# The product of q with k^T v by two 64-row halves of TensorE in two PSUM banks

## The chip, the cores and the metric

The kernel runs on one core of a Trainium2 chip. Its engines run side by side: TensorE (PE in the profile, its weight loads PEld), VectorE (DVE), ScalarE (ACT), GpSimd (POOL) and SyncE (SP), which issues most DMAs. The metric is the device time of one execution in microseconds (us); lower is better. The time before is the median of three runs.

## The reference

Three layers follow one another on 2304 tokens (batch of 4, 8 heads, 576 positions, 64 values a head). The first is a linear attention with an RMS norm, the second and third are MoE layers of plain matrix products.

```python
kv = np.einsum('bhsd,bhse->bhde', k, v)
out = np.einsum('bhsd,bhde->bhse', q, kv)
rms = np.sqrt(np.mean(out * out, axis=-1, keepdims=True) + 1e-06)
x = out / rms * g_norm                                  # to (2304, 512)
h = np.maximum(np.maximum(x @ w1, x @ w2), x @ w3)      # d_ff = 768
x = h @ w_out
for e in range(4):                                      # experts, 1024 wide
    out += p[:, e:e+1] * (np.maximum(x @ ew1[e], 0) @ ew2[e])
```

## The kernel before

Everything is float32. The change lies in the first stage, the attention, which takes some 85 us; the two MoE stages take the rest and are matrix products on TensorE almost without a break.

The 2304 tokens form ten groups. Eight are full (0, 1, 3, 4, 5, 6, 8, 9): 256 positions of one batch, two for each partition. Groups 2 and 7 are pair groups: the last 64 positions of two batches, 128 tokens. For each batch, `att_kv` (steps K, line 282) accumulates k^T v of each head, 64x64, in PSUM bank 7; copies bring it to SBUF as `kvb`. `att_T` (steps T, line 308) transposes q into `qT`: with two positions to a partition, a tile of 128 partitions holds one head's 64 values of the first position and the 64 values of the second one below them. `att_O` (steps O) multiplies `qT` with `kvb`. In a full group it is one matmul a head (line 332): all 128 rows against a 128x128 block of `kvb` that holds the head's k^T v twice on its diagonal, zeros elsewhere, so that both positions come out side by side. The blocks' zeros are set once by a memset of `kvb` on GpSimd. Heads 0 to 3 go to one PSUM bank and heads 4 to 7 to a second one. A pair group needs one bank (line 324).

On the product follow: squares by ACT from each bank (line 345), sums of them on VectorE (line 346), the root on ACT (`att_N`, line 354), its reciprocal and refinement on VectorE (lines 355 to 358), and the scale, by VectorE, of each bank with the reciprocal (line 365). The product stays in its banks until then. `att_X` (line 374) transposes the scaled tokens, and the result goes with the factor of g_norm to `yT` (lines 378 and 380); `split_x` (line 388) divides it into a high and a low part for the MoE products (`col_mm`, line 260). In between, VectorE converts the MoE weights (lines 232 to 236).

Two things set the order of the work. One is a string of steps, written by hand: each engine runs its instructions in the order in which the steps issue them (a letter and its numbers: O4 is the product of group 4, A000 the first MoE product). The other is the PSUM banks: banks 0 to 3 are handed out in turn to products (`bank("acc")`), banks 4 to 6 in turn to transposes and the first MoE products. In the profile and in the orders below, `bank0_66` to `bank7_73` are the banks 0 to 7.

```python
turn[kind] += 1
return banks[(turn[kind] - 1) % 4 if kind == "acc" else 4 + (turn[kind] - 1) % 3]
```

The products come in the order O1, O0, O3, O2, O4, O6, O5, O8, O7, O9 and take the banks 0 and 1, 2 and 3, 0 and 1, 2, 3 and 0, 1 and 2, 3 and 0, 1 and 2, 3, 0 and 1.

Of the kernel before, what the change touches and what calls it, by code (L numbers as in the profile page):

```python
# [21 lines left out]
def tile_attn_moe_moe2(  # L22
# [23 lines left out]
    nc = tc.nc  # L46
# [139 lines left out]
    place = list(range(N1))  # L186
    place[12], place[22] = 22, 12
# [40 lines left out]
    def conv1(pool, key):  # L228
        cpos[2] += 1
        words = stage.pop(key).bitcast(I32).rearrange("p (n t) -> p n t", t=2)  # L230
        ti = conv[key].bitcast(I32)
        nc.vector.tensor_scalar(out=ti, in0=ti, scalar1=3, scalar2=None, op0=ALU.logical_shift_left)
        nc.vector.scalar_tensor_tensor(
            out=ti, in0=words[:, :, 0], scalar=29, in1=ti, op0=ALU.logical_shift_right, op1=ALU.bitwise_or
        )
        nc.vector.scalar_tensor_tensor(
            out=ti, in0=words[:, :, 1], scalar=-(2**31), in1=ti, op0=ALU.bitwise_and, op1=ALU.bitwise_or
        )


    cpos = [0, 0, 0]

    def conv2(key, eng="ap"):
        w, t = new_w(key), conv.pop(key)
        split_h(w, t, eng[0])
        split_l(nc.gpsimd if eng[1] == "p" else nc.vector, w, t, key)
        if key[0] == "a":
            nc.sync.dma_start(out=w_d[key], in_=t)

    def load_w_to(pool, n):  # L250
        while cpos[0] < min(n, N1):
            load_w(pool, worder[cpos[0]])
            cpos[0] += 1
# [18 lines left out]
    def att_kv(kvb, b, c, eng=""):  # L272
# [22 lines left out]
    def att_T(pool, gi, eng="aa"):  # L295

# [4 lines left out]
        if pair:  # L301
            qr = pool.tile([P, 2, H, D], F32, tag="qr", name="qr", bufs=1)
            nc.gpsimd.tensor_copy(out=qr, in_=qs.rearrange("p h r d -> p r h d"))
        for i in range(2):
# [4 lines left out]
            copy(eng[i], t[:, :, :, i] if pair else t[:, i], ps)  # L309
        qT[gi] = t  # L310

    def att_O(pool, kvb, gi):
        b, s0, _ = groups[gi]
        qt = qT[TAIL] if s0 is None else qT.pop(gi)
        ps = [bank("acc") for i in range(1 if s0 is None else 2)]
        xt = pool.tile([P, 2, H, D], F32, tag="xt", name=f"xt{gi}", bufs=3)
        if s0 is None:
            nbank = 1
            for c in range(NPAIR):
                for bb in range(2):  # L320
                    rows = slice(bb * HALF, (bb + 1) * HALF)
                    toks = slice((b + bb) * P // B, (b + bb + 1) * P // B)
                    pair = kvb[(b + bb) % 2][:, 2 * c * P : 2 * c * P + 384]
                    nc.tensor.matmul(
                        ps[0][rows, c * P : (c + 1) * P], qt[:, c, toks, :],
                        pair.rearrange("p (h n) -> p h n", h=2)[:, :, 0:D], start=True, stop=True,
                    )
            dst = [xt[:, 0]]
        else:
            nbank = 2  # L330
            for h in range(H):
                nc.tensor.matmul(
                    ps[h // 4][:, h % 4 * P : (h % 4 + 1) * P], qt[:, h // 4, h % 4, :],
                    kvb[b % 2][:, h * P : (h + 1) * P], start=True, stop=True,
                )
# [939 lines left out]
```

## Time and profile before

| | |
|---|---|
| median of 3 runs | 1098.17 us (1097.75 to 1099.57) |
| profiled execution, its own time | 1097.36 us |
| span of its trace | 1095.6 us |
| mean granted clock of TensorE | 0.994 |
| busy: PE, PEld, DVE, ACT, POOL | 98%, 96%, 70%, 54%, 20% of the span |

The rows of the trace name an engine, a line of the kernel, the operation with its output and input, and the time in us. A wait stands in brackets behind a row, with what ended it. Matmuls overlap, so the length of a row of several is its stretch from the first to the last end. A float32 matmul appears as two passes, each with its weight load. A shape such as `128*64 128x64` gives the rows and columns of the tile of TensorE, and then the output or the operand.

### The profile page before, as it was taken

How to read it: one execution, taken by the hardware profiler on the slowest of the kernel's cores; microseconds unless marked ns; L12 is line 12 of the kernel's file. 1: busy time of each engine (PE TensorE's matmuls, PEld its weight loads, DVE VectorE, ACT ScalarE, POOL GpSimd, SP SyncE). 2: the span in 40 equal slices, each digit the busy share in tenths (PEclk: the TensorE clock that was granted, in tenths of full speed). 3: DMA queues.
4: the chain of work that ended last, by engine and by line, in shares of the span. 5: the costliest groups of instructions: out<-in, count | busy, mean ns of one | idle time of the engine just before them, and what ended most of it. 6: DMA issues, size and time to landing. Idle time of an engine off the chain costs nothing.

```text
span 1095.6 us, 19209 instructions
## 1 busy us (share of the span) xinstructions
PE 1069.1 (98%) x7318; PEld 1051.1 (96%) x7318; DVE 765.7 (70%) x1424; ACT 593.8 (54%) x1257; POOL 221.9 (20%) x269
## 2 busy tenths in 40 slices
PE   7889999999999889999999999999999999999998
PEld 7789999999999789999999999999999999999997
DVE  3889985667656878776766666667677576666556
ACT  3554234435343767665665666666566566556652
POOL 1334422330101101112111211212212220221121
PEclk8999999999999999999999999999999999999999
DMA  9955545431511977288579579659849956956875
GB/s 258 302 157 186 152 177 207 141 116 35 196 58 49 343 262 285 91 316 251 87 242 268 104 193 281 163 117 289 230 77 296 266 88 225 276 113 166 234 223 116
DMA packets 109820, 209.17 MB, mean 191 GB/s; under 512 B 13856, under 2 KB 67104, under 8 KB 109728
## 3 DMA queue, kind: packets, MB, share of 16 engines
q1 hardware_dynamic: 89248, 169.34, 46.3%
q0 software_dynamic: 19472, 37.76, 19.4%
q8 instruction: 57, 0.93, 0.3%
q10 hardware_dynamic: 1008, 0.85, 0.3%
q14 instruction: 35, 0.29, 0.1%
HBM read 137.93 MB, written 69.99 MB: 190 GB/s over the span
## 4 chain that ended last, share of the span: by engine, by line
PE 63%; DVE 0%; issue 0%; DVEq 0%
PE bank L877 32%; PE bank L616 31%; DVE wr L578 0%; DVE xr L499 0%; DVE fa L860 0%; DVE hr L652 0%; DVE hr L650 0%; DVEq L1270 0%
## 5 line engine op out<-in xcount | busy, mean ns | idle before, releaser
L877 PE MATMUL bank<-wr 128*128 128x256 f32 x1701 | 263.5, 283 | 0.4 <-DVE wr L578 0.4
L877 PEld LDWEIGHTS bank<-wr 128*128 128x128 f32 x1701 | 239.8, 190 | 0.6 <-DVE wr L578 0.6
L616 PE MATMUL bank<-rb,wl 128*128 128x384 f32 x1032 | 211.7, 341 | 4.4 <-DVE rb L499 2.5
L670 ACT ACTIVATE fa<-bank 128x384 f32<-128x384 f32 x192 | 94.7, 493 | 171.4 <-PE bank L616 169.5
L616 PEld LDWEIGHTS bank<-rb,wl 128*128 128x128 f32 x1032 | 176.1, 189 | 7.7 <-DVE rb L499 3.7
L616 PE MATMUL bank<-xr,wl 128*128 128x384 f32 x864 | 175.9, 338 | 1.7 <-DVE xr L499 1.1
L616 PEld LDWEIGHTS bank<-xr,wl 128*128 128x128 f32 x864 | 144.9, 188 | 3.7 <-DVE xr L499 2.5
L652 DVE TENSOR_TENSOR wr<-fa,wr 128x384 fp32r<-128x384 f32 x131 | 72.5, 553 | 50.8 <-ACT wr L645 50.6
L877 PE MATMUL bank<-wr,hr 128*128 128x256 f32 x558 | 91.1, 281 | 0.0
L835 POOL DMA_DIRECT2D out_dram<-w2s x48 | 48.1, 1027 | 190.4 <-DVE ob L860 143.4
L835 POOL DMA_DIRECT2D out_dram<-ob x48 | 47.7, 1033 | 170.8 <-DVE w2s L860 89.8
L877 PEld LDWEIGHTS bank<-wr,hr 128*128 128x128 f32 x558 | 80.6, 189 | 0.0
L645 ACT ACTIVATE wr<-fa 128x384 fp32r<-128x384 f32 x152 | 78.2, 529 | 2.0 <-DVE fa L660 0.5
L877 PE MATMUL bank<-wr,xr 128*128 128x256 f32 x405 | 67.9, 281 | 0.0
L759 DVE TENSOR_TENSOR fa<-bank,fa 128x384 f32<-128x384 f32 x54 | 30.0, 555 | 51.3 <-ACT fa L756 36.0
L693 DVE TENSOR_TENSOR fa<-bank,fa 128x384 f32<-128x384 f32 x48 | 26.8, 558 | 49.0 <-PE bank L616 49.0
L682 DVE TENSOR_TENSOR fa<-bank,fa 128x384 f32<-128x384 f32 x48 | 26.8, 558 | 48.0 <-ACT fa L670 47.1
L858 ACT ACTIVATE ob<-bank,p_all 128x256 f32<-128x256 f32 x102 | 48.4, 474 | 21.7 <-PE bank L877 20.0
L858 ACT ACTIVATE w2s<-bank,p_all 128x256 f32<-128x256 f32 x104 | 49.3, 475 | 18.6 <-PE bank L877 18.6
L616 PE MATMUL bank<-op,wl 128*128 128x384 f32 x288 | 58.7, 339 | 0.6 <-ACT fa L670 0.6
L835 POOL DMA_DIRECT2D out_dram<-fa x37 | 34.2, 1054 | 123.3 <-DVE fa L860 69.5
L877 PEld LDWEIGHTS bank<-wr,xr 128*128 128x128 f32 x405 | 59.0, 188 | 0.0
(206 smaller groups left out, 2020.6 us busy)
## 6 DMA issues: line engine op xcount, KB each, us to landing
rb<-op_d SPq DMA_DIRECT2D x42, 768.0 KB, 4.7
xr<-op_d SPq DMA_DIRECT2D x42, 768.0 KB, 6.6
out_dram<-w2s POOLq DMA_DIRECT2D x47, 256.0 KB, 5.8
out_dram<-ob POOLq DMA_DIRECT2D x46, 256.0 KB, 5.4
op<-op_d SPq DMA_DIRECT2D x14, 768.0 KB, 7.8
stage_a<-in_moe_w_dram SPq DMA_DIRECT2D x18, 512.0 KB, 4.0
w1s<-in_moe_w_dram SPq DMA_DIRECT2D x30, 256.0 KB, 3.6
out_dram<-fa POOLq DMA_DIRECT2D x30, 256.0 KB, 6.0
```

Source lines behind the costliest of these rows:

```text
L616: nc.tensor.matmul(out, w[wi][:, c * P : (c + 1) * P], y[yi][:, c, :], start=(i == 0 and k in begin), stop=(i == 5), skip_group_check=k no ...
L645: nc.scalar.activation(out=ops[key][0], in_=src, func=AF.Relu if relu else AF.Copy)
L652: nc.vector.tensor_tensor(out=lo, in0=src, in1=f32(hi), op=ALU.subtract)
L670: nc.scalar.activation(out=out, in_=in_, func=func)
L682: nc.vector.tensor_tensor(out=t22, in0=x, in1=t22, op=ALU.add)
L693: nc.vector.tensor_tensor(out=t12, in0=x, in1=t12, op=ALU.add)
L759: nc.vector.tensor_tensor(out=mx[done] if i == 0 else t, in0=x, in1=t, op=ALU.add)
L835: nc.gpsimd.dma_start(out=rows, in_=src, accum_op=ALU.add)
L858: nc.scalar.activation(out=o, in_=piece(ps, i), func=AF.Copy, scale=pe)
L877: nc.tensor.matmul(piece(ps, i), h[hi][:, i * P : (i + 1) * P], w[wi], start=fresh, stop=last, skip_group_check=True,)
```

## The change

In a full group each head's product is now two matmuls, each on 64 rows of TensorE: the first position of all tokens on rows 0 to 63 into the first bank, the second on rows 64 to 127 into the second bank, one after the other in turn. `kvb` no longer has blocks with zeros: it holds each k^T v in both halves of the partitions, 128x512, by as many copies as before, and the two memsets are gone. A pair group uses two banks as well: even heads go to the first, odd heads to the second, by tiles of 64 rows and 64 columns; its square, sum and scale become two each, of 128x256. The result of the scale is written in the order of the tokens, contiguous. `bank("acc")` is called twice by each pair group, so the turn of the banks shifts: O1, O0, O3, O2, O4, O6, O5, O8, O7, O9 take the banks 0 and 1, 2 and 3 alternately.

The string of steps is written out in smaller steps (the square by O, the sum o, the root N, the refinement m n r, the scale M, and so on, loads included). The instructions keep the order that they had on each engine, the loads of SP too, but for what follows from the counts above; the load of g_norm now stands ahead of the first loads of v on ACT's queue. Three buffers of MoE weights move to a tile `wx` of their own, and the swap of two buffers (`place`) is gone.

```diff
-    place = list(range(N1))
-    place[12], place[22] = 22, 12
...
-        if c == NPAIR - 1:
-            dst = kvb[b % 2][:, 0 : H * P].rearrange("p (c h n) -> p c h n", h=2, n=P)
-            for h in range(2):
-                src = ps[h * D : (h + 1) * D, 0 : NPAIR * D].rearrange("p (c e) -> p c e", e=D)
-                e = eng[2 * h :] or "aa"
-                copy(e[0], dst[0:D, :, h, 0:D], src)
-                copy(e[1], dst[D:P, :, h, D:P], src)
+    def att_J(kvb, b, eng="aaaa"):
+        dst = kvb[b % 2].rearrange("p (c h e) -> p c h e", h=2, e=D)
+        for h in range(2):
+            src = kv_ps[b][h * D : (h + 1) * D, 0 : NPAIR * D].rearrange("p (c e) -> p c e", e=D)
+            for i in range(2):
+                copy(eng[2 * h + i], dst[i * D : (i + 1) * D, :, h, :], src)
 
...
     def att_O(pool, kvb, gi):
         b, s0, _ = groups[gi]
-        qt = qT[TAIL] if s0 is None else qT.pop(gi)
-        ps = [bank("acc") for i in range(1 if s0 is None else 2)]
+        pair = s0 is None
+        qt = qT[TAIL] if pair else qT.pop(gi)
+        ps = [bank("acc") for i in range(2)]
         xt = pool.tile([P, 2, H, D], F32, tag="xt", name=f"xt{gi}", bufs=3)
-        if s0 is None:
-            nbank = 1
+        half = [slice(i * D, (i + 1) * D) for i in range(2)]
+        if pair:
             for c in range(NPAIR):
-                for bb in range(2):
-                    rows = slice(bb * HALF, (bb + 1) * HALF)
-                    toks = slice((b + bb) * P // B, (b + bb + 1) * P // B)
-                    pair = kvb[(b + bb) % 2][:, 2 * c * P : 2 * c * P + 384]
+                for i in range(2):
+                    for bb in range(2):
+                        toks = slice((b + bb) * P // B, (b + bb + 1) * P // B)
+                        nc.tensor.matmul(
+                            ps[i][half[bb], c * D : (c + 1) * D], qt[half[i], c, toks, :],
+                            kvb[(b + bb) % 2][half[i], (2 * c + i) * D : (2 * c + i + 1) * D], start=True, stop=True,
+                        )
+        else:
+            for h in range(H):
+                for i in range(2):
                     nc.tensor.matmul(
-                        ps[0][rows, c * P : (c + 1) * P], qt[:, c, toks, :],
-                        pair.rearrange("p (h n) -> p h n", h=2)[:, :, 0:D], start=True, stop=True,
+                        ps[i][:, h * D : (h + 1) * D], qt[half[i], h // 4, h % 4, :],
+                        kvb[b % 2][half[i], h * D : (h + 1) * D], start=True, stop=True,
                     )
-            dst = [xt[:, 0]]
-        else:
-            nbank = 2
-            for h in range(H):
-                nc.tensor.matmul(
-                    ps[h // 4][:, h % 4 * P : (h % 4 + 1) * P], qt[:, h // 4, h % 4, :],
-                    kvb[b % 2][:, h * P : (h + 1) * P], start=True, stop=True,
-                )
-            dst = [xt[:, :, 4 * i : 4 * i + 4, :].rearrange("p r h d -> p h r d") for i in range(2)]
-        o = [ps[i].rearrange("p (n d) -> p n d", d=D) for i in range(nbank)]
-
-        def small(nm):
-            return smp.tile([P, nbank, 8], F32, tag=nm, name=f"{nm}{gi}")
-
-        ss = small("ss")
-        for i in range(nbank):
-            sq = xt[:, i]
-            nc.scalar.activation(out=sq, in_=o[i], func=AF.Square)
-            nc.vector.reduce_sum(out=ss[:, i, :], in_=sq, axis=AX.X)
-        xtok[gi] = (xt, ss, o, dst, small)
-
-    def att_N(gi):
-        xt, ss, o, dst, small = xtok[gi]
-        nbank = len(o)
-        s0, rr = small("s0"), small("rr")
-
+        n = 4 if pair else 8
+        dst = [xt[:, 0].rearrange("p (c h) d -> p h c d", h=2)[:, i] if pair else xt[:, i] for i in range(2)]
+        o = [ps[i][:, : n * D].rearrange("p (h d) -> p h d", d=D) for i in range(2)]
+        for i in range(2):
+            nc.scalar.activation(out=dst[i], in_=o[i], func=AF.Square)
+
+        xtok[gi] = [xt, o, dst] + [smp.tile([P, 2, n], F32, tag=nm, name=f"{nm}{gi}") for nm in ("ss", "s0", "rr")]
+
+    def att_sum(gi):
+        dst, ss = xtok[gi][2:4]
+        for i in range(2):
+            nc.vector.reduce_sum(out=ss[:, i, :], in_=dst[i], axis=AX.X)
+
+    def att_root(gi):
+        ss, s0, rr = xtok[gi][3:]
         nc.scalar.activation(out=s0, in_=ss, func=AF.Sqrt, scale=1.0 / D, bias=eps)
         nc.vector.reciprocal(out=rr, in_=s0)
-        nc.vector.scalar_tensor_tensor(out=rr, in0=ss, scalar=EPS * D, in1=rr, op0=ALU.add, op1=ALU.mult)
-        nc.vector.scalar_tensor_tensor(out=rr, in0=rr, scalar=1.0 / D, in1=s0, op0=ALU.mult, op1=ALU.add)
-        nc.vector.reciprocal(out=rr, in_=rr)
-        for i in range(nbank):
-            by = rr[:, i, :].unsqueeze(2).to_broadcast([P, 8, D])
-            src = o[i]
-            if nbank == 2:
-                by = by.rearrange("p (h r) d -> p h r d", r=2)
-                src = src.rearrange("p (h r) d -> p h r d", r=2)
-            nc.vector.tensor_tensor(out=dst[i], in0=src, in1=by, op=ALU.mult)
...
-        kvb = [att.tile([P, H * P + P], F32, name=f"kvb{i}", bufs=1) for i in range(2)]
-        for t in kvb:
-            nc.gpsimd.memset(t, 0.0)
...
+        kvb = [att.tile([P, H * D], F32, name=f"kvb{i}", bufs=1) for i in range(2)]
...
-            "K00 K01 c0 d0 K02 K03 T1.va O1 T0.vv N1 K10 K11 O0 X1 N0 T2 T3.va K12 K13.vvaa X0.va O3 S0.pv "
-            "N3 O2 K20 T4 O4 s0.pp N2 T5 N4 K21 c1 T6.av K22 c2 K23 X2 X3 d1 d2 O6 O5 s1.pp K30 s2.pp N6 N5 "
+            "K13 J1.vvaa Lk30 X0 x0.va O3 o3 S0.p z0.v N3 m3 n3 r3 M3 O2 o2 K20 T4 t4 O4 o4 s0.p l0.p N2 m2 n2 "
+            "r2 M2 T5 t5 N4 m4 n4 r4 M4 K21 Lk31 Lq8 Lw3 Lq9 c1 T6 t6.av K22 c2 K23 J2 X2 x2 X3 x3 d1 e1 g1 Lw4 "
...
```

The first place is TensorE's order at the product of group 4 (its q in `qT4`), behind a k^T v product and two transposes of q. Before:

```order
L282 MATMUL bank7_73<-v2_0_276,k2_0_273 64x64 x10
L308 MATMUL bank4_70<-ident_74,q4_239 128x128 x4
L308 MATMUL bank5_71<-ident_74,q4_239 128x128 x4
L332 MATMUL bank3_69<-kvb1_174,qT4_500 128x128 x4
L332 MATMUL bank0_66<-kvb1_174,qT4_500 128x128 x4
L308 MATMUL bank6_72<-ident_74,q5_241 128x128 x4
```

And after the change:

```order
L322 MATMUL bank3_69<-kvb1_178,qT2_407 64x64
L280 MATMUL bank7_73<-v2_0_278,k2_0_275 64x64 x10
L305 MATMUL bank4_70<-ident_74,q4_241 128x128 x4
L305 MATMUL bank5_71<-ident_74,q4_241 128x128 x4
L329 MATMUL bank0_66<-kvb1_178,qT4_538 128x64
L329 MATMUL bank1_67<-kvb1_178,qT4_538 128x64
```

Before, O4 filled bank 3 first and then bank 0; now its matmuls write the banks 0 and 1 in turn.

The second place is TensorE's order at the product of group 9, between MoE products of the first weights (`xr`, `wl`). Before:

```order
L260 MATMUL bank4_70<-xr_81,wl_83 128x384 x12
L260 MATMUL bank5_71<-xr_81,wl_83 128x384 x12
L332 MATMUL bank0_66<-kvb1_174,qT9_785 128x128 x4
L332 MATMUL bank1_67<-kvb1_174,qT9_785 128x128 x4
L260 MATMUL bank6_72<-xr_81,wl_83 128x384 x12
L374 MATMUL bank4_70<-ident_74,xt7_853 128x128 x4
```

And after the change:

```order
L322 MATMUL bank1_67<-kvb0_177,qT2_407 64x64
L322 MATMUL bank1_67<-kvb1_178,qT2_407 64x64
L258 MATMUL bank4_70<-xr_81,wl_83 128x384 x12
L258 MATMUL bank5_71<-xr_81,wl_83 128x384 x12
L329 MATMUL bank2_68<-kvb1_178,qT9_846 128x64
L329 MATMUL bank3_69<-kvb1_178,qT9_846 128x64
```

O9 went to banks 0 and 1, and now goes to banks 2 and 3, in turn.

The third place is VectorE's order at the scales of group 3 (`xt3`), with the sums of groups 2 and 4 behind them. Before:

```order
L357 SCALAR_TENSOR_TENSOR rr3_470<-rr3_470,s03_469 128x16
L358 RECIPROCAL rr3_470<-rr3_470 128x16
L365 TENSOR_TENSOR xt3_453<-bank0_66,rr3_470 128x4x2x64
L365 TENSOR_TENSOR xt3_453<-bank1_67,rr3_470 128x4x2x64
L346 TENSOR_REDUCE ss2_487<-xt2_478 128x8
L346 TENSOR_REDUCE ss4_520<-xt4_511 128x8 x2
```

And after the change:

```order
L356 SCALAR_TENSOR_TENSOR rr3_492<-rr3_492,s03_491 128x16
L358 RECIPROCAL rr3_492<-rr3_492 128x16
L364 TENSOR_TENSOR xt3_471<-bank0_66,rr3_492 128x512
L364 TENSOR_TENSOR xt3_471<-bank1_67,rr3_492 128x512
L344 TENSOR_REDUCE ss2_523<-xt2_504 128x4 x2
L344 TENSOR_REDUCE ss4_568<-xt4_549 128x8 x2
```

The scales of group 3 read banks 0 and 1 in both; the sum of pair group 2 is two smaller ones now. The scales of group 8, which O9 meets on its banks, read banks 1 and 2 before and banks 2 and 3 now.

## Rows read from the trace of the kernel before

**Rows 1.** The page: busy time by engine, and the chain that ended last by line.
```profile
PE 1069.1 (98%) x7318; PEld 1051.1 (96%) x7318; DVE 765.7 (70%) x1424; ACT 593.8 (54%) x1257; POOL 221.9 (20%) x269
...
PE bank L877 32%; PE bank L616 31%; DVE wr L578 0%; DVE xr L499 0%; DVE fa L860 0%; DVE hr L652 0%; DVE hr L650 0%; DVEq L1270 0%
```

**Rows 2.** Windows: us; busy PE, PEld, DVE, ACT, POOL (count); PEclk, DMA share, GB/s.
```profile
12.00:20.00 8.00, 7.49 (x65) 6.73 (x66) 3.08 (x5) 2.71 (x6) 0.00 (x0) 0.61 1.16 285
...
44.00:52.00 8.00, 7.22 (x92) 6.42 (x88) 7.47 (x18) 6.11 (x14) 2.44 (x4) 1.00 1.11 327
...
100.00:120.00 20.00, 19.13 (x109) 18.81 (x108) 19.42 (x29) 6.55 (x12) 8.64 (x10) 1.00 0.63 198
...
384.00:388.00 4.00, 3.21 (x16) 3.01 (x16) 4.00 (x7) 1.75 (x3) 0.00 (x0) 0.73 0.52 201
```

**Rows 3.** Timeline, groups 3 and 4: start, length (us), engine, line, operation, count [idle before].
```profile
34.00 1.64 PEld L332 LDWEIGHTS bank<-kvb,qT 128*128 128x128 f32 x14 [0.57 <-ACT kvb L69]
...
35.60 0.69 DVE L346 TENSOR_REDUCE ss<-xt 128x8 f32<-128x512 f32 x1 [1.74 <-ACT xt L345]
...
35.76 0.85 PEld L324 LDWEIGHTS bank<-kvb,qT 128*64 128x64 f32 x16
...
35.87 0.60 ACT L345 ACTIVATE xt<-bank 128x512 f32<-128x512 f32 x1 [0.30 <-PE bank L332]
...
36.50 0.69 DVE L346 TENSOR_REDUCE ss<-xt 128x8 f32<-128x512 f32 x1 [0.21 <-ACT xt L345]
...
40.52 2.14 PE L332 MATMUL bank<-kvb,qT 128*128 128x128 f32 x16 [0.25 <-ACT qT L69]
...
40.69 1.29 DVE L365 TENSOR_TENSOR xt<-bank,rr 128x512 f32<-128x512 f32 x2
...
43.33 0.69 DVE L346 TENSOR_REDUCE ss<-xt 128x8 f32<-128x512 f32 x1 [0.16 <-ACT xt L345]
```

**Rows 4.** Timeline of VectorE, 44 to 61 us.
```profile
44.87 0.69 DVE L365 TENSOR_TENSOR xt<-bank,rr 128x512 f32<-128x512 f32 x1
...
47.75 0.68 DVE L71 COPY qT<-bank 128x512 f32<-128x512 f32 x1
...
60.59 0.42 DVE L71 COPY kvb<-bank 64x256 f32<-64x256 f32 x1
```

**Rows 5.** Timeline of TensorE, 62 to 125 us.
```profile
62.11 1.14 PE L374 MATMUL bank<-ident,xt 128*128 128x128 f32 x8 [1.47 <-ACT qT L69]
...
80.72 0.63 PE L374 MATMUL bank<-ident,xt 128*128 128x128 f32 x4 [0.77 <-DVE xt L365]
...
115.56 9.78 PE L260 MATMUL bank<-xr,wr 128*128 128x384 f32 x54 [0.87 <-DVE fa L404]
```

**Rows 6.** Timeline, passes of the products: O1, the pair group O2, k^T v.
```profile
23.01 1.86 PEld L332 LDWEIGHTS bank<-kvb,qT 128*128 128x128 f32 x16
...
35.76 1.09 PE L324 MATMUL bank<-kvb,qT 128*64 128x128 f32 x16
...
46.80 0.63 PE L282 MATMUL bank<-v,k 128*64 128x64 f32 x14
```

**Rows 7.** Groups of weight loads by form, 0 to 130 us: busy us, mean ns.
```profile
L282 PEld LDWEIGHTS bank<-v,k 128*64 128x64 f32 x256 | 8.8, 137 | 7.3 <-DMA v<-in_v_dram 5.0 <-issue 1.7
...
L282 PEld LDWEIGHTS bank<-v,k 64*64 64x64 f32 x64 | 3.2, 135 | 1.1
```

**Rows 8.** Line 332: duration in ns, min/median/max, first and last start.
```profile
L332 PEld LDWEIGHTS bank<-kvb,qT x128: 185/192/334, 16.4 to 77.5; 128*128 128x128 f32 x128
```

**Rows 9.** Timeline, groups 8 and 9: VectorE and weight loads, 75 to 78 us.
```profile
75.95 1.29 DVE L365 TENSOR_TENSOR xt<-bank,rr 128x512 f32<-128x512 f32 x2
...
76.69 0.97 PEld L332 LDWEIGHTS bank<-kvb,qT 128*128 128x128 f32 x8 [0.20 <-DVE xt L365]
```

**Rows 10.** Timeline of TensorE, two places where it stood idle.
```profile
12.24 1.97 PE L282 MATMUL bank<-v,k 128*64 128x64 f32 x40 [2.65 <-DMA v<-in_v_dram]
...
384.42 0.62 PE L616 MATMUL bank<-rb,wl 128*128 128x384 f32 x2 [2.32 <-DVE rb L499]
```

More of the change, by code (lines that the diff above doesn't have):

```diff
@@ L270, in tile_attn_moe_moe2, with att_kv @@
     kv_ps = {}
-    def att_kv(kvb, b, c, eng=""):
+    def att_kv(b, c):
         if c == 0:
@@ L301, in att_T @@
         if pair:
-            qr = pool.tile([P, 2, H, D], F32, tag="qr", name="qr", bufs=1)
+            qr = pool.tile([P, 2, 4, P], F32, tag="qT", name="qr", bufs=2).rearrange("p r c (h d) -> p r (c h) d", d=D)
             nc.gpsimd.tensor_copy(out=qr, in_=qs.rearrange("p h r d -> p r h d"))
+        got = []
         for i in range(2):
@@ L370, in att_X, with att_scale @@
+    def att_scale(gi):
+        xt, o, dst, _, _, rr = xtok[gi]
+        for i in range(2):
+            by = rr[:, i, :].unsqueeze(2).to_broadcast([P, rr.shape[2], D])
+            nc.vector.tensor_tensor(out=dst[i], in0=o[i], in1=by, op=ALU.mult)
+    def att_X(gi):
+        xt = xtok.pop(gi)[0].rearrange("p r h d -> p r (h d)")
         t0 = groups[gi][2]
+        got = []
         for r in range(1 if groups[gi][1] is None else 2):
@@ L911, in tile_attn_moe_moe2 @@
         xq = xq_cm.__enter__()
+        wx = ctx.enter_context(tc.tile_pool(name="wx", bufs=1, side="right")).tile([P, 3 * 2 * DM], F32R, name="wx")
+        w_buf.extend(part(wx, n * 2 * DM, 2 * DM, 2) for n in range(3))
         att_cm = tc.tile_pool(name="att", bufs=2, side="right")
@@ L952, in tile_attn_moe_moe2 @@
         nc.gpsimd.tensor_scalar(out=g2, in0=gn, scalar1=2.0, scalar2=None, op0=ALU.mult)
-        xs = []
+        xs = {}
         hidden = {}
         acc = None
+        got = {}
+        left = {"O": len(groups), "X": len(groups)}
         def new_acc(n):
@@ new lines, in tile_attn_moe_moe2 @@
+            at = [int(st[1:])] if kind in "cdegsl" else [int(x) for x in st[1:]]
+            if kind in "cdegsl":
+                key = worder[at[0]]
+                if kind == "c":
+                    conv0(cvp, key)
+                elif kind in "deg":
+                    conv1(key, "deg".index(kind))
+                elif kind == "s":
+                    got["s", key] = conv2h(key, *en)
+                else:
+                    conv2l(key, got.pop(("s", key)), *en)
+            elif kind in "TX":
+                got[kind.lower(), at[0]] = att_T(xq, *at) if kind == "T" else att_X(*at)
+                if kind == "X":
+                    left["X"] -= 1
+                    if not left["X"]:
+                        xq_cm.__exit__(None, None, None)
+                        rp = ctx.enter_context(tc.tile_pool(name="rp", bufs=1, side="right", reuse_waits="tile"))
+                        late["r"] = rp.tile([P, 3 * KT + HK], F32R, name="rb")
+                        late["op"] = rp.tile([P, KT], F32R, name="op5")
+            elif kind in "tx":
+                for e, (dst, src) in zip((en or ["aa"])[0], got.pop((kind, at[0]))):
+                    (copy if kind == "t" else put_x)(e, dst, src)
```

173 lines of the change are left out of this document (82 added, 91 removed), and 23 rows, old and new, of the table steps.

## The prediction

> **What bounds the kernel now.** I read the page first: TensorE is busy 98% of the span, and the chain that ended last is two MoE lines of PE [rows 1]. An edit in the attention stage, the first 85 us, can therefore only move the start of that long run of matmuls. The busy times by stretch say what paces these 85 us. In 12 to 20 and in 44 to 52 us the DMA share is 1.16 and 1.11: the inputs still stream in. But in the second stretch VectorE is busy 7.47 of 8 us, and in 100 to 120 us 19.42 of 20 [rows 2], and PE waits on it or on what stands behind it at 62.11 (1.47), 80.72 (0.77) and 115.56 (0.87) [rows 5]. So a microsecond saved on PE in this stage is worth little, and a microsecond by which VectorE falls behind is worth much. The timeline around groups 3 and 4 shows where VectorE has slack: it waits 1.74 us for the squares of group 3 at 35.60, 0.21 at 36.50 and 0.16 for the square of group 4 at 43.33 [rows 3]; from there to the copy of kvb that ends at 61.01 its rows name no wait [rows 4]. The changed product stands ahead of exactly these squares.
>
> **The product itself.** Today a full group costs 8 matmuls of 128 rows by 128 columns, 16 passes in the trace (fp32 takes two): 1.86 us of weight loads for 16, the last of them 0.19, so (1.86−0.19)/15 = 0.111 us a pass and 1.78 us a group [rows 6, 8]. The change makes 32 passes of 64 rows, 128 weight columns and 64 moving columns. No row of before has that tile, so its cost is bounded from both sides.
> - Column halves do run side by side. The pair group (64 weight columns, 128 moving) takes (1.09−0.27)/15 = 0.054 a pass (a matmul's own 0.27 at the end), so 0.109 for two; with 64 moving columns as well, k^T v takes (0.63−0.22)/13 = 0.031, or 0.063 for two [rows 6].
> - What sets 0.111 for a full group? A load takes 192 ns at 128 columns [rows 8], 137 at 64 columns with 128 rows, and 135 at 64 columns with 64 rows [rows 7]. So a load goes by its columns and not by its rows: 55 ns for 64 columns, 0.11 us for 128, which is the pitch. The change halves the rows of a load, keeps its 128 columns and doubles the number of loads.
>
> The Trainium skill speaks for both ends. "TensorE: Matmul & The Clock Gate", section "Step-by-step: what each phase is for", says that load time scales with the column count and that the row count does not matter; the three load rows agree, and by it the halves would gain nothing. "TensorEngine Tiling (Array Packing)", section "Theoretical Speedup", gives up to 2x where a side is 64 or less; by it a group would take about 0.9 us.
>
> Lower bound: both halves at the pitch of the fastest pair seen, 16×0.063 = 1.0 us. Upper: every load in turn, 32×0.111 = 3.55. I take the loads of two halves side by side, each as long as a 128-column load: 16×0.111 = 1.78, no gain; this is nearest to the load rows. To it comes the change of tile shape: the loads of the full group O3 end at 35.64, those of the pair group behind it start at 35.76 [rows 3], while loads of one shape overlap by 0.08 (192 ns long, one each 111): 0.20 us a change. A full group now has two such changes where no other tiled product stands next to it, 0.3 to 0.4 us of PE, and 0 as the lower bound.
>
> **When the banks are ready.** Before, four heads fill the first bank and four the second, so the first square starts at half the product. At O3 the second square starts at 35.87 and VectorE's second sum ends at 37.19 [rows 3]. Now the halves alternate and both banks are whole only at the end. The first square starts when the second did, the second 0.6 later (a square's time); with a change of shape ahead of it the second sum ends at about 37.85. That is +0.65 for all behind it, the scales of group 3 included: they ended at 41.98 [rows 3] and now end at 42.63.
>
> **The banks in turn.** A pair group now takes two of the four banks. Before, O4's first bank was the spare one, so O4 began at 40.52 while VectorE's scales of group 3 ran from 40.69 [rows 3]. Now O4 takes the two banks that these scales read, and since both are written from the first instructions on, it waits for the second scale: 42.7. Its product ends at 44.5, the first square starts at about 44.8, the second ends at 46.1, the second sum at about 46.8 instead of 44.02: **+2.75** on VectorE. Queued behind these sums on VectorE are the scales of groups 2 and 4, the copies of qT and kvb and the weight conversions; on PE, behind the waiting product, the transposes of groups 5 and 6 and the next k^T v. By the trace none of VectorE's instructions up to 61 waits, so nothing absorbs it. The pair group's halved scale and sum add 0.16 each (64x256 costs 0.42, 128x512 0.68, so two halves cost 0.84 [rows 4]); the sum's share falls before the wait and hides in it, the scale's does not. VectorE is late by about **2.9** at its copy of kvb (60.59), which ACT's copies and then PE's transposes of group 6 (62.11) wait for in a row [rows 4, 5]. PE resumes at 65.0; its work before ended at 60.64 and slips by about 1.5, so it idles some 3 us there.
>
> Next, O9. Before, it started on a bank long free and only its second half waited, 0.20 us, for the first scale of group 8; now it needs both scales, which end at 77.24 [rows 9]. With VectorE 2.9 and once more 0.16 late that is 80.3. Group 7's scale and transposes follow, on VectorE 3.2 late; on PE the 0.77 us wait of before takes up a part. What goes into the run of MoE matmuls is VectorE's lateness, and the wait of 0.87 at 115.56 shows that VectorE still leads there [rows 5]. **+3.2.**
>
> **What costs nothing.** The two memsets of kvb on GpSimd go, but PE's first products wait for v (2.65 us before 12.24 [rows 10]); the memsets covered nothing. The scale's output becomes contiguous with the same 128x512 elements; the pair group's, contiguous before, took 0.69 [rows 4] where two of the others took 1.29 [rows 3], so no change. The finer steps leave the order on every engine as it was, apart from the load of g_norm, now ahead of v on ACT's queue: it is hidden while the inputs stream, and a slip of v would show in the wait at 12.24. Weight buffers move to other tiles in the same order; I cost that at nothing.
>
> **The sum.** Profiled execution 1097.36 + 3.2 = 1100.6, and the median of the runs shown lies 0.81 above that execution: 1101.4. The clock is a term of its own. After PE's idle of 2.65 us at 12.24 the mean granted clock is 0.61 in 12 to 20 us, and after one of 2.32 at 384.42 it is 0.73 in 384 to 388 [rows 2, 10], a mix of the levels 2.4 and 1.2 GHz. An idle of 3 us before 65 may cost the like: 4 us at 0.73 lose 1.1. Not being sure of it, I put in 0.4: **1101.8**, its own range 1100 to 1104. A change under 0.2% (2.2 us) can hardly be told from none by the runs.
>
> **The rivals.**
> - *The halves load one after the other* (slower, 0.15). For it: the 0.111 pitch is that of the loads, and their number doubles; against it: column halves load side by side [rows 6]. O3's second sum is +2.4 (0.65 and 1.78), O4's +6.2 (its product ends at 48), and O8 and O9 add up to 1.8 each, part of it beside VectorE: about +9, 1107, from 1104 to 1109.
> - *The halves really halve the product* (0.18): 1.0 us a group. For it: column halves do just that [rows 6]. Both banks are then ready when the first was, O3 costs 0, and O4 still waits for group 3's scales at 41.98: product to 43.0, squares 43.3 to 44.5, second sum to 45.2: +1.2, with two halved scales +1.5: 1099.7, no change that can be told. It decides from a pitch below 0.08 for two halves on.
> - *The bank waits don't bite* (the other side: not slower, 0.12). VectorE's density before 62 us would be no bound of its own, since the inputs stream in until then [rows 2]; its lateness would vanish against later loads. PE then sees only its own work: O8 and O9 at the lower bound 0.5 to 0.8 shorter each, the pair group likewise: at best −1.4, 1096.8. It decides where PE's idle before the transposes of group 6 stays at 1.47.
> - *The change doesn't do what it says*, in that the work on PE does not shrink: this is my forecast (0.55), 1101.8.
>
> **How the numbers follow.** Slower: 0.55 less 0.04 that falls under the bound, 0.15, and 0.02 of the halving: 0.68. Same: 0.04, 0.14 of the halving and 0.06 of the last rival: 0.24. Faster: 0.02 and 0.06: 0.08. The range runs from 1098.5, which leaves out most of the bank rival, to 1106.5, which cuts the serial case in its lower half.
>
> **What would show it.** Right: weight loads of a full group at 0.055 a pass, 32 of them in 1.8 us; O4 starting at 42 to 43 behind group 3's second scale; VectorE's second sum of O4 ending near 46.8; the transposes of group 6 at 64 to 66 with a longer wait before them; O9 at about 80 behind group 8's second scale. Wrong: a pass at 0.03 (halving) or 0.11 (serial); O4 at 41; the transposes of group 6 still at 62. If they land at 65 and the end still does not move, slack later in the MoE took it up, and my reading that VectorE leads at 115 us fails.

## The result and the profile after

The changed kernel takes 1105.73 us (median of 5 runs, 1104.19 to 1109.77) against 1099.05 before (5 runs): ratio 1.0072, 95% interval 1.0045 to 1.0100. The ratio is taken from all runs and makes 7.9 us; the two medians differ by 6.7. The kernel is slower, as forecast, but by about twice the forecast 3.6 us. The execution that was profiled is one of its slowest (1109.72 us, span 1107.9, mean granted clock 0.981), so its rows show the losses near their largest; a second profile, below, shows the same stretches.

The page of the changed kernel, busy times and the chain by line:

```profile
PE 1081.0 (98%) x7478; PEld 1062.3 (96%) x7478; DVE 764.7 (69%) x1428; ACT 593.9 (54%) x1259; POOL 218.1 (20%) x267
...
PE bank L884 32%; PE bank L623 30%; DVE wr L585 0%; DVE xr L506 0%; DVE fa L867 0%; DVE hr L659 0%; DVE hr L657 0%; DVEq L1283 0%
```

Nothing changed in what bounds the long part [rows 1]: busy PE grew by 12 us and the span by 12. The busy times by stretch say where (us; busy PE, PEld, DVE, ACT, POOL; granted clock, DMA share, GB/s):

```profile
12.00:20.00 8.00, 7.38 (x78) 6.19 (x80) 0.69 (x1) 2.11 (x5) 0.00 (x0) 0.50 1.08 280
28.00:36.00 8.00, 8.00 (x56) 7.78 (x56) 3.08 (x8) 3.90 (x7) 1.04 (x1) 0.54 1.13 273
44.00:52.00 8.00, 4.66 (x41) 4.31 (x40) 5.50 (x12) 2.83 (x7) 0.00 (x0) 0.81 1.11 294
86.00:92.00 6.00, 6.00 (x40) 5.88 (x41) 4.55 (x12) 1.92 (x4) 1.65 (x3) 0.54 0.40 134
100.00:120.00 20.00, 20.00 (x119) 19.89 (x119) 17.60 (x29) 7.87 (x14) 8.06 (x9) 1.00 0.64 194
```

The reader is to see the clock column. Before, it was 0.61 in 12 to 20 and 1.00 from 22 on. Now the clock is at the lower of its two levels (1.2 of 2.4 GHz) for most of 12 to 36 us, again behind the wait at O4 and again in 86 to 92, with TensorE busy without a gap in two of these stretches. VectorE, dense before, is busy 5.50 of 8 us in 44 to 52: its longest wait there, 2.29 us at 50.66 below, is for the square of the late product.

The timeline of TensorE and VectorE around O3, the two bank waits and the transposes behind them:

```profile
39.32 2.04 PEld L329 LDWEIGHTS bank<-kvb,qT 64*128 64x128 f32 x28 [0.18 <-ACT kvb L69]
...
41.96 1.28 DVE L344 TENSOR_REDUCE ss<-xt 128x8 f32<-128x512 f32 x2 [2.38 <-ACT xt L337]
...
46.43 1.29 DVE L364 TENSOR_TENSOR xt<-bank,rr 128x512 f32<-128x512 f32 x2
47.27 3.13 PE L329 MATMUL bank<-kvb,qT 64*128 64x64 f32 x32 [3.24 <-DVE xt L364]
50.66 1.28 DVE L344 TENSOR_REDUCE ss<-xt 128x8 f32<-128x512 f32 x2 [2.29 <-ACT xt L337]
...
58.88 3.86 PE L329 MATMUL bank<-kvb,qT 64*128 64x64 f32 x64
...
70.66 1.15 PE L373 MATMUL bank<-ident,xt 128*128 128x128 f32 x8 [1.28 <-ACT qT L69]
...
74.02 2.00 PE L329 MATMUL bank<-kvb,qT 64*128 64x64 f32 x32
...
79.07 0.69 PE L322 MATMUL bank<-kvb,qT 64*64 64x64 f32 x32
...
85.24 0.43 PE L329 MATMUL bank<-kvb,qT 64*128 64x64 f32 x2 [1.11 <-DVE xt L364]
85.84 3.09 PE L329 MATMUL bank<-kvb,qT 64*128 64x64 f32 x30 [0.17 <-DVE xt L364]
88.86 4.21 PE L258 MATMUL bank<-xr,wl 128*128 128x384 f32 x12
```

Both waits came, O4's with 3.24 us and O9's with 1.11, and 0.17 more for the second bank [rows 3, 9]. Behind them the 32 passes of O4 take 3.13 us and the last 30 of O9 3.09, where 32 passes at the full clock take 2.00 (at 74.02). The MoE product behind O9 takes 4.21 where it took 2.33 before. The transposes of group 6 start at 70.66, 8.55 later than before [rows 5]. But 5.74 of that are there before O4: the scales of group 3 start at 46.43, not 40.69 [rows 3]. Where they come from shows at the start, in TensorE's timeline:

```profile
9.44 0.69 PE L280 MATMUL bank<-v,k 128*64 128x64 f32 x16 [2.72 <-DMA v<-in_v_dram]
12.60 4.86 PE L280 MATMUL bank<-v,k 64*64 64x64 f32 x64 [2.48 <-DMA v<-in_v_dram]
17.39 1.97 PE L305 MATMUL bank<-ident,q 128*128 128x128 f32 x8
19.38 3.68 PE L329 MATMUL bank<-kvb,qT 64*128 64x64 f32 x32
```

The first k^T v starts at 9.44 and not at 7.77, there are two waits for v where there was one [rows 10], and O1 and behind it O0 run at half clock, 3.68 us each. (In the kernel before only O1, at 16.45, ran so, in 3.75 us; the product at 23.01 in [rows 6], 2.05 us long, is O0.)

The product at the full clock, in a row: 64 passes in 3.86 us, (3.86−0.27)/63 = 0.057 a pass, 0.114 for two halves, 1.82 us a group. Its loads, from the list of line 329 (ns, min/median/max), are as long as with 128 rows [rows 8]:

```profile
L329 PEld LDWEIGHTS bank<-kvb,qT x256: 182/188/335, 19.4 to 88.4; 64*128 64x128 f32 x128
```

### The profile page after: what moved, and what is told of

The parts are those of the page before. It is cut to its first block, busy times and chain, and to the rows that moved or that the text cites. A ratio compares the mean times of both kernels' runs of the same rounds, so it can differ in the third digit from the quotient of the medians.

```text
span 1107.9 us, 19532 instructions
## 1 busy us (share of the span) xinstructions
PE 1081.0 (98%) x7478; PEld 1062.3 (96%) x7478; DVE 764.7 (69%) x1428; ACT 593.9 (54%) x1259; POOL 218.1 (20%) x267
## 4 chain that ended last, share of the span: by engine, by line
PE 62%; DVE 0%; issue 0%; DVEq 0%
PE bank L884 32%; PE bank L623 30%; DVE wr L585 0%; DVE xr L506 0%; DVE fa L867 0%; DVE hr L659 0%; DVE hr L657 0%; DVEq L1283 0%
## 5 line engine op out<-in xcount | busy, mean ns | idle before, releaser
L884 PE MATMUL bank<-wr 128*128 128x256 f32 x1521 | 239.7, 283 | 0.0
L884 PEld LDWEIGHTS bank<-wr 128*128 128x128 f32 x1521 | 216.5, 190 | 0.0
L659 DVE TENSOR_TENSOR wr<-fa,wr 128x384 fp32r<-128x384 f32 x117 | 64.6, 552 | 43.3 <-ACT wr L652 43.1
L652 ACT ACTIVATE wr<-fa 128x384 fp32r<-128x384 f32 x134 | 69.4, 528 | 1.7 <-DVE fa L667 0.5
```

Of the source, the lines that this page charges most:

```text
L652: nc.scalar.activation(out=ops[key][0], in_=src, func=AF.Relu if relu else AF.Copy)
L659: nc.vector.tensor_tensor(out=lo, in0=src, in1=f32(hi), op=ALU.subtract)
L884: nc.tensor.matmul(piece(ps, i), h[hi][:, i * P : (i + 1) * P], w[wi], start=fresh, stop=last, skip_group_check=True,)
```

## Experiments

Ratios are to runs of the kernel before on the same chip; 0.001 is 1.1 us. Theory 1: g_norm ahead of v delays the start. Theory 2: the row halves keep the granted clock low once it has fallen (2a by their 64 moving columns, 2b by the 64-row tile). Theory 3, that of the prediction: the waits for banks.

**One part undone, or one part alone.**

*g_norm late*: in the changed kernel, the load of g_norm behind the first loads of q.

```diff
-        for h in range(2):            # ahead of all steps
-            nc.scalar.dma_start(out=gn[h * D : (h + 1) * D, :], ...)
+                if st == "Lq2":       # in the loop over steps
+                    for h in range(2):
+                        nc.scalar.dma_start(out=gn[h * D : (h + 1) * D, :], ...)
```

> The changed kernel with the load of g_norm behind the first loads of q, k and v again, as it stood before. Theory 1 (load order): g_norm ahead of v makes TensorE wait twice for v (2.72 and 2.48 us), and the granted clock falls to 0.50 until 34.6 us. Then the first product starts at 7.8 instead of 9.44, the clock is back by 21 to 23, the k^T v at 36.06 stands at 31, and the time falls by 4 to 6 us, to 1099 to 1101. Theory 2 (the row halves keep the clock down once it has fallen): one wait for v of 2.6 us stays, the clock stays at 0.50 well past 21, and at most 2 us come back: 1103 to 1105. Theory 3 (the bank waits at O4 and O9 are the loss): 1104 to 1106 as now.

Measured 1.0032 (1.0017 to 1.0047), 1103.89 us. Some 4 us come back, but TensorE still has long stretches of half clock (mean granted clock 0.982 to 0.990 over its 12 runs, 0.989 to 0.996 over those of the kernel before); 3.5 us remain.

*Full rows*: in the changed kernel, `kvb` with blocks and zeros, and in full groups the matmul and scale of before; pair groups unchanged. (To make room, one weight buffer moves from `wx` to `wr`.)

```diff
-            for h in range(H):
-                for i in range(2):
-                    nc.tensor.matmul(ps[i][:, h * D : (h + 1) * D], qt[half[i], h // 4, h % 4, :], ...)
+            for h in range(H):
+                nc.tensor.matmul(ps[h // 4][:, h % 4 * P : (h % 4 + 1) * P], qt[:, h // 4, h % 4, :],
+                                 kvb[b % 2][:, h * P : (h + 1) * P], start=True, stop=True)
```

> The changed kernel with the full groups' product on 128 rows against blocks with zeros again (memset of kvb included); pair groups by tiles of 64 rows in two banks, the turn of the banks and the early load of g_norm stay. Theory 1 (load order): nothing of the early loss comes back, the clock is at 0.50 to 30 or later, 1103 to 1106. Theory 2 (row halves keep the clock down): both waits for v stay but the clock is back some 6 us after them, by about 21; 4 us come back, 1100 to 1102. Theory 3 (bank waits): the first half of a product needs one bank alone, so O4 starts some 0.6 us sooner: 1103 to 1105.

Measured 1.0014 (1.0004 to 1.0025), 1100.96 us: four fifths of the loss are in what this takes back, the row halves of the full groups and the two banks they fill, together with the layout of `kvb` and of the scale.

*g_norm early*: the kernel before, with the load moved ahead.

```diff
+        for h in range(2):
+            nc.scalar.dma_start(out=gn[h * D : (h + 1) * D, :], ...)
         order = (
...
         pump()
-        for h in range(2):
-            nc.scalar.dma_start(out=gn[h * D : (h + 1) * D, :], ...)
```

> The kernel before with nothing but the load of g_norm issued ahead of the first loads of v. Theory 1 (load order): the first product at 9.4 instead of 7.77, two waits for v, the clock at 0.50 for 10 us or more, and the time rises by 3 to 6 us, to 1102 to 1105. Theory 2 (row halves keep the clock down): the waits come, but the full-row product brings the clock back by 21; plus 1 to 2 us at most. Theory 3: no change within 1 us.

Measured 1.0013 (1.0003 to 1.0022), 1100.95 us: plus 1.4 us, the same as the kernel with full rows, which has g_norm early too. In this timeline the waits of the changed kernel are there:

```profile
9.18 0.69 PE L282 MATMUL bank<-v,k 128*64 128x64 f32 x16 [2.09 <-DMA v<-in_v_dram]
12.23 4.97 PE L282 MATMUL bank<-v,k 64*64 64x64 f32 x64 [2.37 <-DMA v<-in_v_dram]
```

*Turn*: the kernel before, a pair group draws two banks and uses one.

```diff
-        ps = [bank("acc") for i in range(1 if s0 is None else 2)]
+        ps = [bank("acc") for i in range(2)]
```

> The kernel before with the turn of the banks alone shifted: a pair group takes two of the four banks and uses one. Theory 3 (bank waits): O4 waits for the first scale of group 3, O9 for the first scale of group 8, and the time rises by 2 to 3 us, to 1100 to 1102. Theories 1 and 2: the first half of O4 waits 0.8 us only for the first scale and the second half is not later than before, so under 1 us.

Measured 1.0000 (0.9988 to 1.0011). O4 waits 1.02 us and O9 0.88 for the scales in this profile, and the time does not move. The shifted turn alone costs nothing. The kernel with full rows says the same: O4 waits 1.20 us and O9 1.30 in its profile, and it takes no longer than *g_norm early*.

**The clock.** *Wide halves*: in the changed kernel, 128 moving columns; the second 64 are those of the next head and are written over by its own matmul.

```diff
+                    to = min(h + 2, H) * D
                     nc.tensor.matmul(
-                        ps[i][:, h * D : (h + 1) * D], qt[half[i], h // 4, h % 4, :],
-                        kvb[b % 2][half[i], h * D : (h + 1) * D], start=True, stop=True,
+                        ps[i][:, h * D : to], qt[half[i], h // 4, h % 4, :],
+                        kvb[b % 2][half[i], h * D : to], start=True, stop=True,
                     )
```

> The changed kernel with 128 instead of 64 moving columns in each row-half matmul of a full group: head h also writes the columns of head h+1, which the next matmul writes over. Nothing else differs; tile shape, loads, waits and the early load of g_norm stay. Theory 2a (the granted clock stays low because the half tiles keep TensorE streaming only half of the time, the loads setting the pitch): the pitch of a pair stays at 0.11 us at the full clock, the columns now fill it, the clock is back by about 21 and does not fall at O4 and O9, and the time is that of the full rows, 1100 to 1102. Theory 2b (the 64-row tile itself keeps the clock down, whatever streams through it): clock and time as the changed kernel, 1104 to 1107.

Measured 1.0040 (1.0027 to 1.0052), 1102.68 us. TensorE's timeline near the start:

```profile
12.43 4.95 PE L280 MATMUL bank<-v,k 64*64 64x64 f32 x64 [2.71 <-DMA v<-in_v_dram]
...
19.29 2.00 PE L330 MATMUL bank<-kvb,qT 64*128 64x128 f32 x32
```

The wait for v is as long as in the changed kernel and the k^T v behind it as slow, but O1 is back at the full clock. (The clock falls once more, to 0.50 in 30 to 32 us, and is back by 34.) A pass takes what a narrow one takes there (32 in 2.00 us), though it moves twice the columns. To have both on one chip, each was run again:

> The changed kernel once more, beside its wide variant on the same chip and with a second profile, because its first one fell on the slowest of its five runs. Theory 2: 1104 to 1107, and in the profile one or more stretches of half clock of 10 us and longer, at other places than in the first profile where an execution differs.

> The changed kernel with the wide row halves once more, on the same chip as the changed kernel. Theory 2a: 2.5 to 4 us under it, stretches of half clock of some 6 us at most. If streaming did not matter: the same time as the changed kernel.

Narrow 1.0064 (1.0050 to 1.0077), 1105.66 us; wide 1.0032 (1.0020 to 1.0045), 1102.44 us. By the ratios, 3.5 us between them, and every narrow run takes longer than every wide one (1104.09 at least, 1102.77 at most). The mean granted clock says the same in all ten runs: 0.981 to 0.986 narrow, 0.989 to 0.991 wide (0.991 to 0.997 for the kernel before). Busy times by stretch, the narrow kernel first; the profiled executions, of 1110.75 and 1101.49 us, lie further apart than the 3.5 us:

```profile
20.00:36.00 16.00, 15.98 (x131) 14.79 (x131) 6.59 (x17) 5.29 (x11) 1.04 (x1) 0.50 1.18 249
36.00:56.00 20.00, 16.61 (x215) 14.46 (x214) 13.90 (x31) 9.04 (x20) 3.92 (x4) 0.84 1.00 255
80.00:100.00 20.00, 18.77 (x141) 18.00 (x141) 17.04 (x38) 7.57 (x16) 7.76 (x10) 0.83 0.24 69
```

and the wide one:

```profile
20.00:36.00 16.00, 12.14 (x174) 10.34 (x172) 10.43 (x22) 6.96 (x14) 1.04 (x1) 1.00 1.15 257
36.00:56.00 20.00, 16.39 (x270) 14.45 (x266) 15.41 (x32) 11.71 (x26) 6.86 (x7) 1.00 1.12 298
80.00:100.00 20.00, 20.00 (x143) 19.75 (x143) 18.34 (x38) 8.91 (x16) 8.24 (x10) 1.00 0.52 157
```

In the wide kernel the clock column is 1.00 in all three (in 12 to 20 us it is 0.59); in the narrow one TensorE is busy through 20 to 36 and stays at 0.50. The transposes of group 6 in the wide kernel:

```profile
64.97 1.15 PE L374 MATMUL bank<-ident,xt 128*128 128x128 f32 x8 [2.20 <-ACT qT L69]
```

*Two streams*, with no wait in them, in place of the first 16 matmuls of the kernel before (their times are not compared):

```diff
-        for _ in range(WARM):
-            nc.tensor.matmul(banks[3][:, 0:P], ident, ident, start=True, stop=True)
+        for _ in range(150):
+            for i in range(2):
+                half = slice(i * D, (i + 1) * D)
+                nc.tensor.matmul(banks[2 + i][:, 0:64], ident[half, :], ident[half, 0:64], start=True, stop=True)
```

and the same with 128 in place of 64 columns.

> The kernel before, with its 16 identity matmuls at the start replaced by 150 pairs of row-half matmuls, 64 moving columns each, one half in either of two banks, with no wait between them: a stream of 600 passes from a cold engine. Its time says nothing, only the pitch of the passes. Theory 2a (half streaming keeps the clock from coming back): the pitch stays at 0.11 us a pass for much longer than the 3 to 5 us in which the identity matmuls reach the full clock, 10 us or more, or for all 66 us. Theory 2b's and theory 1's reading (streaming does not matter to the clock): 0.11 for about 4 us, then 0.056, 36 us in all.

> The same with 128 moving columns in each half. Theory 2a: 0.11 us a pass for some 4 us, then 0.056, about 36 us in all. Theory 2b (the 64-row tile keeps the clock down): as the narrow stream, 0.11 for 10 us or more.

TensorE's timeline, narrow and then wide, each with the k^T v behind it:

```profile
1.34 64.27 PE L918 MATMUL bank<-ident 64*128 64x64 f32 x600 [1.34 <-POOL ident masks.py:199]
65.54 5.91 PE L282 MATMUL bank<-v,k 128*64 128x64 f32 x80
```

```profile
1.35 36.69 PE L918 MATMUL bank<-ident 64*128 64x128 f32 x600 [1.35 <-POOL ident masks.py:199]
37.96 3.58 PE L282 MATMUL bank<-v,k 128*64 128x64 f32 x80
```

The same number of passes on the same tile, one execution each. The narrow stream takes 64.27/600 = 0.107 us a pass, about the pitch of the changed kernel's product at a clock of 0.50 (32 passes in 3.68, (3.68−0.27)/31 = 0.110), and the k^T v behind it still runs slow (5.91). The wide one takes 36.69, 0.061 a pass on average, and the k^T v behind it runs at 3.58. The clock column shows 1.00 through both streams and behind them, so here the level is read from the pitch alone. On one tile the 64 columns stay slow and the 128 do not: 2a holds, and 2b falls.

**Waits filled or moved, narrow halves.** *Reorder*: O4 behind T5 and K21, group 2's root and scale ahead of group 4's sums, O9 behind A210.

```diff
-M3 O2 o2 K20 T4 t4 O4 o4 s0.p l0.p N2 m2 n2 r2 M2 T5 t5 N4 m4 n4 r4 M4 K21 Lk31
+M3 O2 o2 K20 T4 t4 T5 t5 K21 Lk31 N2 m2 n2 r2 M2 O4 o4 s0.p l0.p N4 m4 n4 r4 M4
...
-A010 a010 A100 a100 O9 o9 s4.p l4.p A210 a210
+A010 a010 A100 a100 s4.p l4.p A210 a210 O9 o9
```

> The changed kernel with O4 moved behind the transposes of group 5 and the next k^T v, the root and scale of group 2 ahead of the sums of group 4, and O9 behind the MoE product A210. Theory 2 (half tiles lower the clock, a wait ahead of them sets it off): without the waits of 3.2 and 1.1 us the clock does not fall at O4 and O9, the early loss to 34 us stays: minus 2 to 4 us against the changed kernel, 1101 to 1104. Theory 3 (the waits alone, as the prediction had it): minus 3, the same number, but then without a change of the clock. Rival: the waits are replaced by others behind them: no gain.

Measured 1.0072 (1.0060 to 1.0084): no gain. O4 still waits 0.98 us, and the early loss is whole.

*Warm*: `WARM = 36` instead of 16.

> The changed kernel with 36 instead of 16 matmuls of the identity at the start, 20 more that fill TensorE's wait for v. They push the first k^T v to about 11, which still lies before the second wait for v ends at 12.6. Theory 2: the clock never falls at 11.7, so the first 24 us of half clock go away: O1 at 17 in 1.8 us, the k^T v at 36.06 stands at 31; minus 3 to 4 us, 1101 to 1103. If the early loss were the late loads of v alone (theory 1), nothing comes back: 1104 to 1106, since v lands as late as before.

Measured 1.0074 (1.0059 to 1.0088): no gain. The clock is at 1.00 up to 24 us as meant, but falls behind the next wait for v (2.55 us, to 23.31), 0.58 in 24 to 32, and O0 takes 3.58 us there. A filled gap gave the loss to the next one.

*Moved*: the split of the first tokens (z0) behind the scales of group 3, one weight conversion behind the scales of group 8.

```diff
-O3 o3 S0.p z0.v N3 m3 n3 r3 M3 O2
+O3 o3 S0.p N3 m3 n3 r3 M3 z0.v O2
...
-S1 z1 d4 e4 g4 Lw7 c5
+S1 z1 c5
...
-r8 M8 d5 e5
+r8 M8 d4 e4 g4 Lw7 d5 e5
```

> The changed kernel with these two moves on VectorE alone; narrow row halves and the early load of g_norm stay. Theory 2a (half streaming lowers the clock where an idle time of 1 us or more stands next to it): without the waits at O4 and O9 the granted clock stays at 1.00 from 36 us on, and 2 to 4 us come back: 1101 to 1104. If the clock falls without a wait, by the half streaming alone: 1104 to 1107.

Measured 1.0040 (1.0028 to 1.0052), 1103.28 us. The waits at O4 and O9 are gone and some 3 us come back, but the clock is at 0.50 in 40 to 52 without a wait at O4, and the transposes of group 7 now wait for their scale. TensorE's timeline at both places, and under it the first of them in the kernel with full rows:

```profile
38.02 0.69 PE L322 MATMUL bank<-kvb,qT 64*64 64x64 f32 x32
40.40 1.53 PE L280 MATMUL bank<-v,k 128*64 128x64 f32 x20 [1.69 <-DMA v<-in_v_dram]
...
43.76 3.68 PE L329 MATMUL bank<-kvb,qT 64*128 64x64 f32 x32
...
87.18 0.63 PE L373 MATMUL bank<-ident,xt 128*128 128x128 f32 x4 [1.77 <-DVE xt L364]
```

```profile
37.52 0.69 PE L323 MATMUL bank<-kvb,qT 64*64 64x64 f32 x32
40.12 0.95 PE L280 MATMUL bank<-v,k 128*64 128x64 f32 x20 [1.90 <-DMA v<-in_v_dram]
```

In these two executions an idle time of 1.69 us behind narrow halves leaves the k^T v at the lower clock (1.53 instead of 0.95), and a longer one behind full rows does not. Others show that this is no rule: the k^T v of *warm* (narrow) at the same place, and O4 in two wide kernels, *the same with the moves* (below) and *wide* run again:

```profile
41.08 0.95 PE L280 MATMUL bank<-v,k 128*64 128x64 f32 x20 [1.82 <-DMA v<-in_v_dram]
```

```profile
42.36 3.97 PE L330 MATMUL bank<-kvb,qT 64*128 64x128 f32 x32 [1.54 <-DVE xt L365]
```

```profile
42.95 2.50 PE L330 MATMUL bank<-kvb,qT 64*128 64x128 f32 x32 [1.94 <-DVE xt L365]
```

Behind 1.82 us and narrow halves the k^T v still runs at the full clock, which falls only in the transposes behind it; of two wide O4 the one behind the shorter wait is the slow one. Full rows are not spared either: in *g_norm early* a wait of 1.30 us at 58.30 is followed, one k^T v later, by transposes that take 1.94 us instead of 1.09.

**Put together.** *Wide and g_norm late*:

> The changed kernel with the wide row halves (128 moving columns) and the load of g_norm behind the first loads: what the change was, less the two causes of a low clock. If the three parts add up (late v about 1.6 us, low clock about 3, late banks the rest), what is left is the banks' part alone: 1.5 to 2.5 us over the kernel before, 1100.5 to 1101.5. If the clock's part was not the streaming but the early gap, this and the kernel with g_norm late alone agree: 4 us over.

Measured 1.0016 (1.0006 to 1.0026), 1100.44 us: 1.8 us remain. *The same with the moves*:

> The kernel of the run before this one, and on VectorE the split of the first tokens moved behind the scales of group 3 and one weight conversion behind the scales of group 8, so that these scales come 2.3 and 2.2 us earlier and O4 and O9 need not wait for them. If the banks' waits are what is left, the time falls to that of the kernel before, 1098 to 1099.5. Rival: VectorE is as dense as before and only its order differs, so the waits go elsewhere and nothing comes back: 1100.5 to 1101.5.

Measured 1.0011 (0.9999 to 1.0022), 1099.83 us: not to be told from the kernel before, nor from the version without the moves. *The moves on the kernel before*:

> The kernel before with the same two moves on VectorE. Its O4 and O9 hardly wait, so by the reading that VectorE's work sets the pace from 44 us on there is nothing to gain: 1098 to 1100. If the earlier scales let TensorE run ahead, 1 us under the kernel before.

Measured 1.0020 (1.0012 to 1.0029): the moves themselves cost 2.2 us there. In the profile (of an execution of 1103.17 us) the transposes of group 7 wait 2.19 us for their scale, where they waited 0.77, and an earlier k^T v waits 1.50 us for v, with lower clock behind both; how much of the 2.2 us that is was not tested. *Full rows, g_norm late and the reordering*:

> The changed kernel with the product on 128 rows against blocks with zeros again, the load of g_norm behind the first loads again, and O4, O9 and the scale of group 2 moved as in the reordered kernel; pair groups stay on 64-row tiles. Theory 2: no half clock but the 6 us after the first wait for v, no wait at O4 and O9: 1098 to 1099.5, the time before. If the waits of before at the same places are worth something, a little under it: 1097.

Measured 1.0023 (1.0014 to 1.0031), 1101.12 us: not the time before, as expected, but 2.5 us more, and why is open. No version beats the kernel before.

## Why the prediction was right and wrong

The direction was right and the bank waits named for it came, but the sum was half of what came. Two terms of it failed.

The first is the term of the clock: "I put in 0.4". It measured 3.5 us (narrow against wide on one chip, 1.0064 and 1.0032). The prediction weighed one idle time of 3 us, before 65, as a trigger. That one was 1.28 us, and the clock is 1.00 in 56 to 80; it fell behind the late v, at O4 and at O9. What was missed is that the changed product itself keeps the clock from coming back.

The second is the load of g_norm, put at nothing since "it is hidden while the inputs stream". Alone it cost 1.4 us; taking it out of the changed kernel gave 3.5 to 4.4 back (1.0064 and 1.0072 to 1.0032), and the longest stretch of half clock, 12 to 34 us in the profile, begins at the late v. Without either cause 1.8 us are left (1.0016), so the two together cost 5.3 to 6.2 us.

That 1105.73 lies inside the stated range is luck: the range was drawn up to 1106.5 for loads one after the other, which did not come, and the forecast's own range ended at 1104.

One way to split the loss, each part uncertain by 1 to 2 us:

| part | forecast, us | measured, us | from |
|---|---|---|---|
| load of g_norm ahead of v | 0 | 1.4 to 1.5 | g_norm early 1.0013; full rows 1.0014 against turn 1.0000 |
| turn of the banks alone | in 3.2 | 0 | turn 1.0000 |
| both banks filled in turn, with that | 3.2 | 2.0 to 2.9 | wide 1.0032 and 1.0040 against full rows 1.0014 |
| narrow halves, the clock | 0.4 | 3.5 | narrow 1.0064 against wide 1.0032 |

The rows are steps from one kernel to the next, so that they add up to the changed kernel (6.9 to 7.9) is no proof of them. Taken in another order they differ: with g_norm late the narrow halves cost 1.8 (1.0032 against 1.0016).

- *The product itself*: right. 0.114 for two halves against 0.111, no gain from 64 rows: loads of 128 columns take 188 ns with half the rows, 192 with all. The Trainium skill's rule ("TensorE: Matmul & The Clock Gate", section "LDWEIGHTS (loading the stationary operand)": the columns of a load set its time, not its rows) agrees with these rows. The Trainium skill's "TensorEngine Tiling (Array Packing)", section "Theoretical Speedup", gives up to 2x where a dimension is 64 or less; full groups show none of it. In pair groups, whose loads have 64 columns, 1.09 us became 0.69.
- *When the banks are ready*: right at O3. From the product's long stretch at 39.32 to the end of the sums at 43.24 the changed kernel takes 3.92 us, where it took 3.19 [rows 3]: +0.73 for the +0.65 forecast.
- *The banks in turn*: right in place and kind, both waits as described; O9's second half starts behind the second scale, at 85.84. The path behind them came out otherwise in the changed kernel: the transposes of group 6, forecast at 64 to 66 behind a longer wait, stand at 70.66 behind a shorter one, and in 100 to 120 us TensorE is busy 20.00 of 20 us where it waited 0.87 us for VectorE before [rows 2, 5]. It is TensorE that is late there. The wide kernel takes the forecast path: 64.97, behind 2.20 us. The price of 2.0 to 2.9 for 3.2 is a difference between kernels that also differ in tiles and in the layout of `kvb` and of the scale, so that the banks alone cost it is argued and not shown. With the first half of the heads in one bank, waits at the same places cost nothing (turn, full rows).
- *What costs nothing*: wrong for g_norm. The prediction names the place, "a slip of v would show in the wait at 12.24", but puts no price on it; v did land later, and a late v makes everything behind it late. For the memsets it was right, though no run leaves them out alone. In the trace of the kernel before they end at 3.32, and the first copy into `kvb` starts at 14.3:

```profile
1.27 2.05 POOL L922 MEMSET kvb<- 128x1152 f32 x2
```

- *The bound of rivals*: serial loads and halved work both fell (0.114, neither 0.22 nor 0.06). That the bank waits don't bite holds for the shifted turn alone.

What stays open: what decides whether the clock falls behind an idle time of 1 to 3 us; why moving VectorE's work costs the kernel before 2.2 us, and why full rows with g_norm late and the reordering cost 2.5; how much of g_norm's 1.4 us is the late start and how much the clock behind it.

## What to carry to other kernels

Splitting a matmul into row halves paid here only where its weight loads got shorter too; a load that kept its 128 columns kept its time (188 and 192 ns). A stage that looks busy without a gap can run at the lower clock, as the 64-column passes did here: read the pitch of the passes, not the busy share. A small load moved to the head of a queue is a change of its own, to be costed against the first thing that waits. And parts that share a stretch, as the late v and the slow clock do, have no price of their own: take them out in more than one order.

## What the runs showed of the hardware

- 600 passes on 64-row tiles with 128 weight and 64 moving columns, without a wait, took 0.107 us a pass for 64 us from the start of the execution; with 128 moving columns they came to 36.69 us in all. TensorE's busy share was 100% in both, and the clock column showed 1.00.
- Doubling the moving columns of a row-half pass from 64 to 128 cost no time at the full clock (32 passes in 2.00 us in both; a load takes 188 ns), and made the whole kernel 3.5 us faster.
- Two row halves do load and run side by side into two banks: 0.114 us for the two, about the time of one 128-row pass (0.111).
- Idle times of like length left TensorE now at one level and now at the other: the same wide product of 32 passes took 3.97 us behind 1.54 us of idle in one execution and 2.50 behind 1.94 in another.
